# A fused convolution and gated MLP: the first block's chain laid anew over the engines, the first weight pieces used for both token halves, loads queued by need, the convolution's output copied from PSUM by ScalarE

## The chip, the cores and the metric

One core of one Trainium2 chip. The metric is the device time of one execution in microseconds (us); lower is better. In the profile PE is TensorE (PEld its weight loads), DVE is VectorE, ACT is ScalarE, POOL is GpSimd, SP is SyncE, which issues nearly all DMAs. A name such as L712 is a line of the kernel.

## The reference

All tensors are bf16, S = 2048 tokens, D = 576, F = 4608.

```python
mod = (silu(c) @ w_mod)                      # six rows of 576: sa, ca, ga, sb, cb, gb
h = layernorm(x) * (1 + ca) + sa             # x is A_q
k_shift = 4-tap causal shift of A_k, taps shift_k
kv = k_shift * A_v
y = causal convolution over all 2048 tokens of kv with ssm_k, per channel (by FFT), + kv * ssm_D
x = x + ga * (h * y)
h = layernorm(x) * (1 + cb) + sb
x = x + gb * ((silu(h @ w1) * (h @ w3)) @ w2)
```

## The kernel before

**Blocks and row blocks.** Tokens go in 8 blocks of 256. The convolution is done per block in a small transform domain: `k_rows` (transpose of the filter's block, L311) and `w_spectrum` give the filter's spectrum W, `v_block` makes V of two neighbouring W, `kv_rows` makes the shifted product kv, `x_spectrum` its spectrum X, `x_sums` one more component, and `pair(X, V, s)` multiplies a block's X with a V and adds the product to block s's accumulator z. A block s needs the pairs of all earlier X, so X and V are kept in DRAM (`Xd`, `Vd`) and read back with `get`. `real_parts` and `inverse` bring z back to tokens (into PSUM), `gate_rows` and `gate` make the modulated layer norm `hg`, `residual` adds `hg * y` to x; then come the second layer norm (`ln_stats`, `normed_act`), `turn` (ten PE transposes) and `turned` (five ACT instructions into `h2T`, the transposed input of the MLP). `outcome` is the sequence from `real_parts` to `turned`.

**The MLP** takes row blocks of 512 tokens (two blocks). `hidden(r, fc, t0, t1, rate)` loads one of nine pieces of w1 and w3 (512 columns of each, `wst`, two buffers, four DMAs) and does four f of 128 columns: 16 matmuls with 128 rows and four with 64, then Silu (L726) and a copy (L728) on ACT and a product on DVE (L729). `down` multiplies by w2 (four buffers, 18 DMAs) into two PSUM tiles and adds to x. There are four PSUM tiles in all (`ps`), shared by everything.

**Order of the work.** `first_block` brings block 0 to `h2T` alone; the order of its DVE, ACT and PE instructions is the program's (`in_order`). In it stand the modulation rows too (`mod_piece` 2, 1, 0, 5 and `mod_columns`). Then `hidden` runs for six pieces on block 0's 256 tokens (`N1 = 24` f) while block 1's convolution (`conv_second`) is interleaved; then row block 0 runs pieces 6 to 8 on 512 tokens and pieces 0 to 5 once more, with weights loaded again, on tokens 256 to 512; then `down`. The convolution of blocks 2r+2 and 2r+3 (`conv`) is interleaved with row block r. The interleaving is by a budget: each step of the convolution yields a cost, `advance` adds a share of time after every f or group of down matmuls (`rate`, from `CONV_US`), and steps are issued while the budget is positive. A negative cost is room that `mix` fills with other steps. Beyond that a scheduler orders instructions when it compiles; it may move an instruction ahead of earlier ones on its engine where its inputs allow.

**Loads.** All large loads are issued by SP. In block 0: k, filter, v, x, then w_mod in two halves (`load_mod`), the next block's filter, k and v, spill of V, x of block 1, weight pieces 0 and 1, spill of X, x of blocks 2 and 3, four pieces of w2. POOL issues c, D and two small pieces of k.

Of the kernel before, what the change touches and what calls it, by code (L numbers as in the profile page):

```python
# [29 lines left out]
CONV_US = (86.5, 93.5, 109.5)  # L30
N1 = 24
# [9 lines left out]
class _Kernel:  # L41
    def __init__(self, ctx, tc, q, k, v, shift_k, ssm_k, ssm_D, w1, w3, w2, c, w_mod, out):
# [21 lines left out]
        self.n_w13 = 0  # L64
# [5 lines left out]
    def setup(self):  # L70
# [51 lines left out]
    def load_mod(self, m):  # L122

        nc = self.nc
        cols = slice(m * D, (m + 3) * D)
        dst = _ap(self.h3, m * D, [[6 * D, 4], [1, 3 * D]])
        nc.sync.dma_start(dst, self.w_mod[0:512, cols].rearrange("(a p) d -> p a d", p=P))
        nc.sync.dma_start(self.wm[0:64, 4 * 6 * D + m * D:4 * 6 * D + (m + 3) * D],
                          self.w_mod[512:D, cols])

    def angles(self, which):

        nc = self.nc
        ang = self.acc.tile([P, 2, 2, 2, P], I32, name="ang", tag=f"z{which}")
        for x in range(2):
            for cs in range(2):
                nc.vector.tensor_scalar(ang[:, x, cs], self.arow_i[:],
                                        self.acol[:, 2 * which + x:2 * which + x + 1],
                                        512.0 * (1 - cs), op0=ALU.mult, op1=ALU.add)
        nc.vector.tensor_single_scalar(ang[:], ang[:], 2047, op=ALU.bitwise_and)  # L140
        self.ang = self.ang if hasattr(self, "ang") else {}
        self.ang[which] = ang

# [41 lines left out]
    def mod_piece(self, m):  # L185
        nc = self.nc
        w5 = self.wm[:, 0:5 * 6 * D].rearrange("p (a d) -> p a d", a=5)
        ps = self.ps()
        for h, ct in [(h, ct) for h in range(2) for ct in range(4)] + [(0, 4), (1, 4)]:
            n = P if ct < 4 else 64  # L190
            nc.tensor.matmul(ps[:, h, 0:H], self.crep[0:n, ct, :],  # L191
                             w5[0:n, ct, m * D + h * H:m * D + (h + 1) * H],
# [34 lines left out]
    def load_kv(self, s, between=None):  # L227
        nc = self.nc
        kh = self.ld.tile([P, 5, D], BF16, name="kh", tag="kh")
        if s == 0:  # L230
# [3 lines left out]
            nc.gpsimd.dma_start(kh[1:2, 1:5, :], bass.AP(tensor=self.k.tensor, offset=self.k.offset,  # L234
                                                       ap=[[2 * D, 1], [D, 4], [1, D]]))
            nc.gpsimd.dma_start(kh[0:1, 3:5, :], bass.AP(tensor=self.k.tensor, offset=self.k.offset,
# [615 lines left out]
```

## Time and profile before

| | us |
|---|---|
| runs (3) | 579.86, 579.95, 580.1; median 579.95 |
| profiled execution | 576.23, of which the span is 574.5 |
| PE busy | 527.4 (92% of the span) |
| DVE busy | 322.5 (56%) |
| ACT busy | 299.0 (52%) |
| POOL busy | 47.7 (8%) |
| mean granted TensorE clock | 0.971 |
| DMA | 121.65 MB, 212 GB/s in the mean |

The largest groups of the page (line, engine, operation; busy us, mean ns):

```profile
L712 PE MATMUL ps<-h2T,wst 128*128 128x512 bf16 (+1 forms) x1314 | 268.7, 352 | 8.5 <-DMA wst<-in_B_w_dram 5.5
L753 PE MATMUL ps<-w2t,h 128*128 128x288 bf16 x1152 | 145.6, 288 | 9.2 <-DVE ty L459 3.4
```

A group's row reads: what it writes and reads, shapes, count, then busy time and mean time of one, then the idle time of the engine just before its instructions and what ended most of that. In the rows of waits, `PE ps L712 <- DMA wst` reads: PE stood before line 712 until a DMA into `wst` had landed. PE's matmuls are pipelined and their ends are modelled, so busy PE time is not time at peak rate.

### The profile page before, as it was taken

The page shows a single profiled execution, that of the slowest core. Times are in us where ns is not written, and L with a number is a line of the kernel's source. Part 1 is how long each engine was busy: PE and PEld are TensorE (multiplying, and loading weights), DVE is VectorE, ACT ScalarE, POOL GpSimd, SP SyncE. Part 2 cuts the span into 40 slices and gives each one's busy share as a digit, 9 for nine tenths or more (in the row PEclk, how much of TensorE's full clock was granted, in tenths as well). Part 3 has the DMA queues.
Part 4 walks back from the last instruction along what each step waited for, and adds up shares of the span by engine and source line. Part 5 has one row for each costly group of instructions (what it writes and reads, how often), then busy time and mean ns, then how long its engine had stood idle before and what let it go on. Part 6 is the DMA issues. An engine that isn't in the chain of part 4 may idle for free.

```text
span 574.5 us, 9033 instructions
## 1 busy us (share of the span) xinstructions
PE 527.4 (92%) x3465; PEld 306.3 (53%) x3496; DVE 322.5 (56%) x496; ACT 299.0 (52%) x627; POOL 47.7 (8%) x107
## 2 busy tenths in 40 slices
PE   5779889999998989999898989999899999999996
PEld 2457554466776634434476744333367843334775
DVE  9569936598676238795496137999453032222011
ACT  5757588655724276557723277455663245555100
POOL 3120010000313010001201010000131000000000
PEclk9959989999998999999999999999989999999999
DMA  9996787597896667976978559745245554452353
GB/s 272 364 280 242 233 244 233 182 342 249 309 337 217 184 211 233 317 260 180 330 247 257 145 175 378 250 149 161 91 121 140 145 165 131 127 154 83 85 153 93
DMA packets 104984, 121.65 MB, mean 212 GB/s; under 512 B 5359, under 2 KB 95215, under 8 KB 104942
## 3 DMA queue, kind: packets, MB, share of 16 engines
q1 hardware_dynamic: 104812, 121.07, 66.4%
q8 instruction: 27, 0.44, 0.3%
q14 instruction: 15, 0.12, 0.1%
q0 software_dynamic: 128, 0.01, 0.0%
q10 hardware_dynamic: 2, 0.00, 0.0%
HBM read 107.20 MB, written 13.86 MB: 211 GB/s over the span
## 4 chain that ended last, share of the span: by engine, by line
PE 56%; DVE 18%; DMA 11%; ACT 9%; issue 3%; POOL 3%; SPq 0%; DVEq 0%; ACTq 0%
PE ps L712 25%; PE ps L753 21%; DMA wst<-in_B_w_dram 6%; PE ps L720 4%; DVE z L365 4%; DVE p L363 4%; PE ps L271 3%; ACT junk L377 3%; DVE h L729 2%; ACT sg L726 1%; ACT u L728 1%; DMA V<-Vd 1%; DMA x<-in_A_q_dram 1%; DMA out_dram<-x 1%; PE ps L191 1%
## 5 line engine op out<-in xcount | busy, mean ns | idle before, releaser
L712 PE MATMUL ps<-h2T,wst 128*128 128x512 bf16 (+1 forms) x1314 | 268.7, 352 | 8.5 <-DMA wst<-in_B_w_dram 5.5
L712 PEld LDWEIGHTS <-wst 128*128 128x128 bf16 x1344 | 126.1, 99 | 135.9 <-issue 26.6
L726 ACT ACTIVATE sg<-ps 128x512 bf16<-128x512 f32 (+1 forms) x168 | 90.2, 537 | 138.9 <-PE ps L720 70.8
L753 PE MATMUL ps<-w2t,h 128*128 128x288 bf16 x1152 | 145.6, 288 | 9.2 <-DVE ty L459 3.4
L729 DVE TENSOR_TENSOR h<-sg,u 128x512 bf16<-128x512 bf16 (+1 forms) x168 | 63.7, 382 | 131.8 <-ACT u L728 131.7
L753 PEld LDWEIGHTS <-h 128*128 128x128 bf16 x1152 | 113.0, 98 | 39.5 <-issue 7.3
L728 ACT CAST u<-ps 128x512 bf16<-128x512 f32 (+1 forms) x168 | 87.7, 522 | 0.0
L377 ACT ACTIVATE junk<-x 128x576 bf16<-128x576 bf16 x60 | 41.4, 690 | 45.0 <-DVE x L461 39.1
L363 DVE TENSOR_TENSOR p<-X,V 128x3456 bf16<-128x3456 bf16 x28 | 54.6, 1950 | 2.6 <-DMA V<-Vd 2.5
L761 DVE TENSOR_TENSOR og<-ps,gbrow 128x288 bf16<-128x288 f32 x32 | 13.1, 449 | 74.5 <-PE ps L753 74.5
L365 DVE TENSOR_TENSOR z<-z,p 128x3456 bf16<-128x3456 bf16 x28 | 54.6, 1949 | 0.0
L720 PE MATMUL ps<-h2T,wst 64*128 64x512 bf16 (+1 forms) x336 | 47.3, 352 | 0.2 <-DVE ty L459 0.2
L271 PE MATMUL ps<-kT,Fk 128*128 128x288 bf16 x128 | 20.0, 304 | 7.9 <-ACT u L728 3.9
L720 PEld LDWEIGHTS <-wst 64*128 64x128 bf16 x336 | 10.0, 94 | 31.7 <-issue 31.1
L493 ACT ACTIVATE h2T<-ps,sbcol,cbcol 128x256 bf16<-128x256 bf16 (+1 forms) x43 | 20.0, 552 | 10.6 <-PE ps L478 9.8
L391 POOL TENSOR_SCALAR l2m<-l2s 128x2 f32<-128x2 f32 x7 | 2.1, 295 | 266.8 <-ACT junk L377 266.8
L271 PE MATMUL ps<-kv,Fb 128*128 128x288 bf16 x128 | 19.8, 300 | 4.6 <-ACT u L728 3.8
L473 ACT ACTIVATE h2row<-x,l2n,l2r 128x576 bf16<-128x576 bf16 (+1 forms) x28 | 16.8, 652 | 11.9 <-POOL l2n L396 11.9
L421 ACT ACTIVATE hg<-x,l1n,l1r 128x576 bf16<-128x576 bf16 x16 | 13.3, 867 | 16.8 <-POOL l1n L396 16.8
L271 PEld LDWEIGHTS <-Fk 128*128 128x128 bf16 x128 | 12.8, 104 | 16.0 <-issue 11.5
L450 PE MATMUL ps<-z,Fb 128*128 128x288 bf16 x128 | 18.2, 295 | 3.0 <-DVE z L440 2.9
L274 ACT CAST W<-ps 128x576 bf16<-128x576 f32 x32 | 19.2, 666 | 2.5 <-PE ps L271 2.5
(94 smaller groups left out, 327.6 us busy)
## 6 DMA issues: line engine op xcount, KB each, us to landing
wst<-in_B_w_dram SPq DMA_DIRECT2D x84, 512.0 KB, 5.0
w2t<-in_B_w_dram SPq DMA_DIRECT2D x72, 288.0 KB, 3.3
X<-Xd SPq DMA_DIRECT2D x12, 864.0 KB, 6.7
V<-Vd SPq DMA_DIRECT2D x10, 864.0 KB, 6.1
Vd<-V SPq DMA_DIRECT2D x7, 864.0 KB, 4.5
wst<-in_B_w_dram SPq DMA_DIRECT2D x84, 64.0 KB, 3.0
Xd<-X SPq DMA_DIRECT2D x6, 864.0 KB, 5.2
kh<-in_A_k_dram SPq DMA_DIRECT2D x7, 720.0 KB, 6.1
```

Of the source, the lines that this page charges most:

```text
L271: nc.tensor.matmul(ps[:, h, 0:H], basis[:, cc, cs, e, :], rhs[:, cc, h * H:(h + 1) * H], start=(cc == 0), stop=(cc == 1))
L274: nc.scalar.copy(dst(e, cs).rearrange("p (h d) -> p h d", h=2), ps[:, :, 0:H])
L363: nc.vector.tensor_mul(p[:], X[:], V[:])
L365: nc.vector.tensor_add(z[:], z[:], p[:])
L377: self.nc.scalar.activation(junk[:], src[:, i, :], func, accum_out=out[:, i:i + 1])
L493: nc.scalar.activation(dst, src, ACT.Identity, bias=self.sbcol[:, ct:ct + 1], scale=self.cbcol[:, ct:ct + 1])
L712: nc.tensor.matmul(gus[fi][:, i, 0:n], w[:, 5 * i + ct, fi * P:(fi + 1) * P], hT[:, ct, t0:t1], start=(first and ct == 0), stop=(not first ...
L720: nc.tensor.matmul(gus[fi][:, i, 0:n], w[rows, 4, fi * P:(fi + 1) * P], hT[rows, 4, t0:t1], start=first, stop=not first)
L726: nc.scalar.activation(sg[:, 0:n], gus[fi][:, 0, 0:n], ACT.Silu)
L728: nc.scalar.copy(u[:, 0:n], gus[fi][:, 1, 0:n])
L729: nc.vector.tensor_mul(self.h3[:, f, t0:t1], sg[:, 0:n], u[:, 0:n])
L753: nc.tensor.matmul(accs[t // 2][:, t % 2, 0:H], self.h3[:, f0 + f, t * P:(t + 1) * P], w[:, f, :], start=(f0 + f == 0), stop=(f0 + f == NF ...
```

## The change

It touches the first block, the stage after it, the order of the loads, and the layer-norm and output steps of every later block.

- **Block 0.** The second set of angles is made by POOL, ahead of the identity. The layer-norm sums of its first 128 tokens come earlier on ACT, those of the other 128 from DVE (`quick_stats`). X's sum, the product with V and the real parts are done in two halves on DVE, ahead of `arow` and `brow`. Six warm-up matmuls are dropped, four added. `k_rows(1)` and half of `w_spectrum(1)` move into block 0's last part; `mod_piece(5)` moves out into block 1's convolution, with a load of its own (`load_gb`). The two halves of `h2T` get PSUM tiles of their own.
- **Weights.** `N1 = 28`: seven pieces run on tokens 0 to 256. Pieces 0 and 1 are loaded right after V of block 0; pieces 5 and 6 are then used at once for tokens 256 to 512 (`kept`), pieces 7 and 8 run on 512 tokens, pieces 0 to 4 are loaded again.
- **Loads.** c and the small pieces of k are issued by SP and ACT. The spills of X and V of blocks 0 and 1 move behind pieces 7 and 8. SP's order up to the end of the first stage is the program's.
- **Every block.** ACT copies the inverse out of PSUM into `y`; DVE's two residual steps work on SBUF, 256 tokens at a time. `behind(nc.scalar)` puts the layer-norm sums, gate rows and normed rows behind the ACT instruction traced just before them. `gate_stats` is split off `gate_rows` and stands earlier.

```diff
-CONV_US = (86.5, 93.5, 109.5)
-N1 = 24
+CONV_US = (84.6, 91.6, 107.6)
+RATE1 = 1.31
+N1 = 28
...
         nc.vector.memset(self.one[:], 1.0)
+        self.ang = {}
+        self.angles(nc.gpsimd, 0)
+        make_identity(nc, self.ident[:])
         nc.gpsimd.memset(self.knat[64:P, 4, :], 0.0)
-        make_identity(nc, self.ident[:])
+        nc.gpsimd.memset(self.h2T[0][:, 0, :], 0.0)
...
-        self.load_kv(0, between=lambda: self.load_k(0))
-        nc.gpsimd.dma_start(self.crow[:], self.c)
+        def between():
+            self.load_k(0)
+            nc.sync.dma_start(self.crow[:], self.c)
+            self.load_x(0)
+        self.load_kv(0, between)
         nc.gpsimd.dma_start(self.drow[:], self.ssm_D.rearrange("(o d) -> o d", o=1))
-        self.load_x(0)
-        self.load_mod(0)
-        self.load_mod(3)
-        nc.gpsimd.memset(self.h2T[0][:, 0, :], 0.0)
+        self.load_mod(0, 3)
+        self.load_mod(3, 2)
...
+    def load_gb(self):
+        self.wgb = self.ld.tile([P, 5, D], BF16, name="kh", tag="kh")
...
+    def behind(self, engine):
+        last = [i for i in self.nc.cur_bb.bb.instructions if i.engine == engine.engine][-1]
+        return self.tc.issue_after(last)
...
+    def residual_row(self, s, cc, ps):            # block 0: as before, from PSUM
...
+    def residual(self, s, y):
+        nc.vector.tensor_mul(hg[:], hg[:], y[:])
+        nc.vector.tensor_add(x1[:], x1[:], hg[:])
...
     def first_block(self):
-        self.angles(1)
-        self.angles(0)
+        self.angles(nc.vector, 1)
+        self.whole_turns(1)
+        self.whole_turns(0)
         self.shift_taps()
         self.waves(1)
+        self.waves(0)
         self.warm(4)
         self.run_all(self.k_rows(0))
-        self.waves(0)
+        self.load_k(1)
+        self.warm(4)
...
         self.cond_silu()
+        self.cond()
+        self.ln_sums(x1, 0, sums[0], sums[1], 0)
+        scales = [self.ln_scales(*sums, "l1")]
         self.run_all(self.w_spectrum(0))
-        self.cond()
         self.run_all(rows)
-        self.ln_sums(self.xo[0], 0, *st)
+        mean, rstd = self.quick_stats(x1[:, 1, :], "l1")
...
         self.run_all(self.x_spectrum(0))
         self.run_all(self.v_block(0))
+        self.load_w13(0)
+        self.load_kv(1)
         self.load_x(1)
-        self.mod_piece(2)
-        self.ln_sums(self.xo[0], 1, *st)
-        for m in (1, 0):
+        self.load_w13(1)
+        for o in (0, 3):
+            nc.vector.tensor_add(X[:, o, :], X[:, o + 1, :], X[:, o + 2, :])
+            nc.vector.tensor_mul(z[:, o:o + 3, :], X[:, o:o + 3, :], V[:, o:o + 3, :])
+            nc.vector.tensor_add(z[:, o + 1, :], z[:, o, :], z[:, o + 1, :])
+            nc.vector.tensor_sub(z[:, o, :], z[:, o, :], z[:, o + 2, :])
+        for m in (2, 1, 0):
             self.mod_piece(m)
-        self.gate_rows(0, self.ln_scales(*st, "l1"))
-        self.run_all(self.x_sums(0))
-        self.run_all(self.pair(self.X[0], self.V[0], 0))
-        self.real_parts(0)
-        self.warm(6)
+        for cc in range(2):
+            nc.scalar.activation(hg[:, cc, :], x1[:, cc, :], ACT.Identity, bias=b[:, 0:1], scale=r[:, 0:1])
+        ps = [self.inverse(0, cc) for cc in range(2)]
         self.run_all(self.gate(0))
-        ps = [self.inverse(0, cc) for cc in range(2)]
         self.mod_columns()
+        self.run_all(self.k_rows(1))
+        W1 = self.w_spectrum(1)
         pt = self.ps((P, 2, 1024), BF16)
-        self.residual(0, 0, ps[0])
+        self.residual_row(0, 0, ps[0])
...
-        self.turn(pt, 0)
+        self.turn_split(pt, 0)
+        for _ in range(2):
+            next(W1)
         st.append(self.quick_stats(x1[:, 1, :], "l2"))
-        self.turned(0, pt, 0, 1)
+        self.turned_split(pt, 0, False)
         self.normed(0, 1, *st[1])
-        self.turn(pt, 1)
-        self.turned(0, pt, 1, 1, True)
-        self.mod_piece(5)
+        pt = self.ps((P, 2, 1024), BF16)
+        self.turn_split(pt, 1)
+        self.turned_split(pt, 1, True)
...
     def outcome(self, s, fill=()):
             self.real_parts(s)
             yield 1.5
             yield -3.5
-            ps = [self.inverse(s, cc) for cc in range(2)]
+            y = self.lnp.tile([P, 2, D], BF16, name="y", tag="y")
+            for cc in range(2):
+                nc.scalar.copy(y[:, cc, :].rearrange("p (h d) -> p h d", h=2), self.inverse(s, cc)[:, :, 0:H])
             yield -3.5
-            for cc in range(2):
-                self.residual(s, cc, ps[cc])
-                yield 1.2
-            r, b = self.ln_stats(self.xo[s], "l2")
+            self.residual(s, y)
+            yield 1.5
+            with self.behind(self.nc.scalar):
+                r, b = self.ln_stats(self.xo[s], "l2")
             yield -4.0
-            self.normed_act(s, r, b)
+            with self.behind(self.nc.scalar):
+                self.normed_act(s, r, b)
...
     def conv_second(self):
-        self.gate_rows(1)
-        yield from self.k_rows(1)
-        yield from self.kv_rows(1)
-        yield from self.w_spectrum(1)
-        yield from self.x_spectrum(1)
-        yield from self.gate(1)
+        self.gate_stats(1)
+        yield from self.W1
+        yield from self.kv_rows(1)
+        self.load_gb()
         yield from self.v_block(1)
+        self.gate_rows(1)
+        yield from self.x_spectrum(1)
+        self.mod_piece(5)
...
+        yield from self.gate(1)
         yield from self.outcome(1)
...
     def run(self):
             for fc in range(n1):
-                self.hidden(0, fc, 0, 256, 39.0 / (N1 * 1.03 * 0.8))
+                self.hidden(0, fc, 0, 256, RATE1)
             self.end()
+        sync = self.nc.sync.engine
+        last = self.in_order(0, [sync])[sync]
+        with self.tc.issue_after(last):
+            self.row_blocks(n1)
...
+    def row_blocks(self, n1):
             if r == 0:
-                for fc in range(n1):
+                self.load_kv(2)
+                self.load_k(2)
+                for fc in (n1 - 2, n1 - 1):
+                    self.hidden(0, fc, 256, 512, rate, self.kept[fc])
+                for fc in range(n1, NF // FC):
+                    self.hidden(0, fc, 0, RB, rate)
+                    self.keep_x(fc % 2)
+                    self.keep_v(fc % 2)
+                for fc in range(n1 - 2):
                     self.hidden(0, fc, 256, 512, rate)
```

More of the change, by code (lines that the diff above doesn't have):

```diff
@@ L348, in v_block @@
         self.V[s] = V
[L349 to L350 removed]
+        if 1 < s < NBLK - 1:
+            self.keep_v(s)
         yield 0.75
@@ L479, in turn, with turn_split, turned_split, turned @@
                                      self.h2row[:, cc, ct * P:(ct + 1) * P], self.ident[:])
-    def turned(self, s, pt, c0, n, split=False):
+    def turn_split(self, pt, cc):
+        for ct in range(5):
+            self.nc.tensor.transpose(pt[:, ct // 3, ct % 3 * P:(ct % 3 + 1) * P],
+                                     self.h2row[:, cc, ct * P:(ct + 1) * P], self.ident[:])
+    def turned_split(self, pt, cc, both):
+        hT = self.h2T[0]
+        for ct in range(5):
+            dst, src = hT[:, ct, cc * P:(cc + 1) * P], pt[:, ct // 3, ct % 3 * P:(ct % 3 + 1) * P]
+            if both and ct > 2:
+                self.nc.vector.tensor_scalar(dst, src, self.cbcol[:, ct:ct + 1], self.sbcol[:, ct:ct + 1],
+                                             op0=ALU.mult, op1=ALU.add)
+            else:
+                self.nc.scalar.activation(dst, src, ACT.Identity, bias=self.sbcol[:, ct:ct + 1],
+                                          scale=self.cbcol[:, ct:ct + 1])
+    def turned(self, s, pt, c0, n):
         nc = self.nc
```

132 lines of the change are left out of this document (79 added, 53 removed).

## The prediction

> **What bounds the kernel now.** I read the busy table by stages first: block 0 alone (to 42.2 us), the first halves of six weight pieces (to 84.2), the rest of row block 0's hidden layer (to 152), its down projection (to 195), then row blocks 1 and 2. Columns: stretch, length, busy us (instructions) of PE, PE's weight loads, DVE, ACT and POOL, granted clock, DMA share, GB/s.
>
> ```profile
> 0.00:42.20 42.20, 28.31 (x187) 17.32 (x188) 29.30 (x56) 24.88 (x48) 9.83 (x29) 0.81 0.98 312
> 42.20:84.20 42.00, 37.58 (x313) 26.04 (x314) 32.06 (x57) 29.04 (x78) 3.08 (x6) 0.95 0.73 235
> 84.20:152.00 67.80, 63.92 (x462) 37.74 (x463) 45.82 (x73) 46.23 (x109) 3.46 (x12) 1.00 0.79 260
> 152.00:195.00 43.00, 39.57 (x319) 30.79 (x318) 28.12 (x35) 15.34 (x35) 10.37 (x12) 0.96 0.81 255
> 195.00:327.00 132.00, 122.89 (x773) 67.88 (x780) 83.44 (x113) 71.93 (x144) 9.83 (x24) 1.00 0.74 244
> 327.00:461.00 134.00, 126.60 (x783) 69.87 (x790) 82.27 (x111) 72.89 (x144) 11.09 (x24) 0.97 0.58 178
> ```
>
> After block 0 TensorE is busy 89 to 95% of every stage, so time can come from two places: block 0, where PE idles 13.9 of 42.2 us and the clock is 0.81, and the waits that PE still has. Those are in the waits of PE over the whole span (total, times, longest):
>
> ```profile
> PE ps L271 <- ACT u L728: 7.7, 5, 2.6
> PE ps L712 <- DMA wst<-in_B_w_dram: 5.5, 8, 1.3
> PE ps L753 <- DVE ty L459: 3.4, 2, 2.6
> ...
> PE ps L753 <- ACT u L728: 2.5, 1, 2.5
> ...
> PE ps L712 <- ACT u L728: 1.0, 1, 1.0
> ```
>
> All but the weight wait are waits for one of the four PSUM tiles: 7.7 + 3.4 + 2.5 + 1.0 = 14.6 us, all after 152 us. The waits of ACT say why its evacuations come late; it executes in order, and layer-norm work stood ahead of them, waiting:
>
> ```profile
> ACT junk L377 <- DVE x L461: 39.1, 8, 13.4
> ...
> ACT hg L421 <- POOL l1n L396: 16.8, 6, 4.7
> ```
>
> **Part 1, block 0.** The chain of waits there (start, length), and DVE's wait in it:
>
> ```profile
> 23.81 0.76 DVE brow L205
> 25.27 1.97 DVE z L358
> 27.26 0.77 DVE z L440
> 28.05 0.76 DVE z L441
> 28.81 0.68 DVE hg L432
> 29.51 0.77 DVE hg L434
> 30.38 0.77 DVE ty L459
> ...
> 37.27 1.75 ACT h2T L493 x5
> 39.07 0.69 PE ps L478 x5
> 39.76 2.51 PE ps L191 x10
> 42.27 1.41 PE ps L712 x8
> ```
> ```profile
> DVE arow L203 <- PE ps L191: 4.3, 1, 4.3
> ```
> ```profile
> 18.75 2.24 ACT L274 CAST X<-ps 128x576 bf16<-128x576 f32 x4
> ```
>
> Now DVE idles 4.3 us for the modulation products while X is ready at 18.75 + 2.24 = 21.0, and only afterwards forms the spectral product. After the change the product stands ahead of `arow` and `brow`, in two halves. Two of the four LN sums leave ACT for DVE and the others come before W's copies; I put the last X copy at 19 to 21. One half costs a sum of half L440's size (0.4), half of L358 (1.0) and two steps of half L440's size (0.8): 2.2. The other half lies beside the X copies, so z is final at 21.2 to 23.2 instead of 28.81. `arow`, `brow` and the two gate steps (4 x 0.76 = 3.0) follow on DVE; the inverse transform runs on PE beside them. The first residual starts at 24.4 to 26.4 instead of 30.38: 4 to 6 us earlier. I take 4.5.
>
> From residual to first hidden matmul it is now 42.2 - 30.4 = 11.8 us. Out go `mod_piece(5)` (2.51) and part of the second turn's wait for ACT (a PSUM tile of its own). In come, on the same in-order engines, block 1's ten transposes, ACT's kT copy and two groups of W(1) with their copies (0.56 each, the X copies' 2.24 / 4; kT is of two such): about 3 on PE at the cold clock, partly in its gaps, and 2.2 on ACT, ahead of ACT's five L493. Net -0.5, between +2 and -3. Dropping six warm-up matmuls and adding four earlier can leave the inverse at half clock as it is today; nothing gained or lost. ACT issues the two small `kh` loads before its first work: nothing. POOL's angles: below.
>
> Sum of part 1: **-5.0** (-1.5 to -7.5); first hidden matmul near 37.
>
> **Part 2, from there to 152.** One unblocked f takes, by the spacing of the Silu rows, 1.09 us for 256 tokens and 2.04 for 512:
>
> ```profile
> 117.78 0.38 ACT L726 ACTIVATE sg<-ps 128x256 bf16<-128x256 f32 x1 [0.34 <-PE ps L712]
> ...
> 118.87 0.38 ACT L726 ACTIVATE sg<-ps 128x256 bf16<-128x256 f32 x1 [0.45 <-PE ps L720]
> ```
> ```profile
> 248.20 0.60 ACT L726 ACTIVATE sg<-ps 128x512 bf16<-128x512 f32 x1 [0.98 <-PE ps L720]
> ...
> 250.24 0.60 ACT L726 ACTIVATE sg<-ps 128x512 bf16<-128x512 f32 x1 [0.97 <-PE ps L712]
> ```
>
> Four more f are split, 4 x (2.18 - 2.04) = +0.5. The ten matmuls of L191 above took 2.51 at half clock, so one takes 0.125 warm, and ten transposes 0.7 (L478: five in 0.69 cold). The convolution's PE work in stage 1 thus loses the transposes and half of W(1), -0.7 - 8 x 0.125, and gains `mod_piece(5)`, 10 x 0.125: -0.5.
>
> Stage 1 idles 42.0 - 37.58 = 4.4 now, and its clock of 0.95 costs some 2.1 more: 6.5, on weights, on LN waits and on cold stretches. What it will lose: SP's queue is now in program order, so piece 2 of w1/w3 (1.18 MB) stands behind the 0.66 MB for `gb`, which waits for `kv_rows(1)` on DVE; at block 0's 312 GB/s both take 6 us against the 5 that PE spends on a piece with its share of convolution: 1, and 0.5 for their issue. Each us that `kv_rows(1)` is late is one more. The step costs sum to 37.65 while 28 advances of 1.343 give 37.6, so the last step (turn and five L493) falls behind the last f, and the second halves that follow need it: five L493 took 1.75 for one half, so about 2.4 for two, 2.5. A cold start: 0.8. In all 4.8 instead of 6.5: -1.7.
>
> Pieces 5 and 6 serve both halves without a reload, so one piece less is read; in exchange four spills (0.88 MB each) come into the third stage. That moved 67.8 us x 260 GB/s = 17.6 MB; +3.5 - 1.2 makes 295 GB/s, under the 312 that block 0 moved. So the spills stay covered, narrowly; without that cover they cost 2.3 MB / 0.3 = 8 us. The weight wait of 5.5 neither grows nor shrinks in my sum.
>
> Sum of part 2: +0.5 - 0.5 - 1.7 = **-1.7** (+2 to -5).
>
> **Part 3, the PSUM waits after 152.** In `outcome` ACT copies the inverse to SBUF (4 x 0.56 more a row block) and DVE works there afterwards, so PSUM no longer waits for DVE's L459 behind 1.95 us products: of 3.4 I take 2.5. LN sums, gate rows and normed rows are bound behind the ACT instruction issued last, so they no longer stand ahead of Silu with a wait of their own. For the other 11.2 I take half, 5.5, since ACT's order is still strict and gains the copies. **-8.0** (-2 to -13). The two planner rates only follow these step costs.
>
> **Sum:** -5.0 - 1.7 - 8.0 = -14.7. The profiled execution took 576.23 (span 574.5 and 1.7 around it): 561.5. The median of the runs lies 3.7 above it: 579.95 - 14.7 = **565.2**. All bounds together give 554.5 to 578.5.
>
> **The rivals.** *POOL is late.* Block 0's second set of angles moves to POOL, ahead of the identity that the transposes need. The rows that bear on it:
>
> ```profile
> 23.43 0.20 POOL L394 TENSOR_TENSOR l1v<-l1v,l1r 128x2 f32<-128x2 f32 x1
> ```
> ```profile
> 281.13 1.95 DVE L363 TENSOR_TENSOR p<-X,V 128x3456 bf16<-128x3456 bf16 x1
> 281.35 1.79 POOL L394 TENSOR_TENSOR l1v<-l1v,l1r 128x2 f32<-128x2 f32 x1
> ```
>
> The same 2-element POOL instruction takes 0.20 alone and 1.79 beside a DVE product, until that ends. If the four angle instructions are held so by DVE's own four, and are slow themselves, the angles end about 2 us later than DVE could use them, and DVE, which masks them before the tap work, idles for that: part 1 shrinks to -3, the time is 567.2. The Trainium skill (SBUF — State Buffer, Who interferes with whom) states it as a lock: VectorE and GpSimd share one port pair, and whoever starts second is blocked for the whole instruction; the trace agrees (1.79 against 0.20).
>
> *Front alone.* The PSUM waits come back elsewhere: PE is fast enough to fill four tiles whenever ACT does any long step. For it: ACT's work grows. Against it: ACT is busy only 54% in the two long stages (71.93 of 132, 72.89 of 134). Gain 5.0 + 1: 574.
>
> *All of it.* The 14.6 nearly vanish and stage 1 flows: -7 - 4 - 14: 555.
>
> *Slower.* The y copy is one more in-order step on ACT that waits for PE's inverse, and that for DVE's z. Today's eight waits of ACT for L461 (39.1, the longest 13.4) show how far such a step can stand still; Silu behind it would stop PE at all seven outcomes. It decides from 14.7 / 7 = 2.1 us each; at 3.5 each the time is 590. Against it: the inverse is issued 3.5 units after `real_parts`, and PE shows no wait for z outside block 0.
>
> **Chances.** Forecast 0.50 (its own range 559 to 571); POOL late 0.15; front alone 0.14; all of it 0.09; slower 0.08; gains and losses cancel to within 0.2% (1.2 us, about what these runs can tell from no change) 0.04. Faster 0.88, same 0.04, slower 0.08. A range of 555 to 575 leaves out about 2 in 10: the slow case, a few of the best, some of the front alone.
>
> **What would show it.** Right: first hidden matmul near 37, z ahead of `arow`, the first halves done near 79 with four more f, no PE wait for a residual, ACT's 39.1 gone. Wrong: PE waits on ACT of over 2 us after an inverse, weight waits over 8 in total, a DMA share near 1 in the third stage, or a hidden start after 40.

## The result, and the profile after

The changed kernel takes 565.01 us (median of 562.72 to 566.88), the kernel before in the same comparison 579.9 (579.44 to 580.1): ratio 0.9742, 95% interval 0.9706 to 0.9779. Its profiled execution took 565.24, the span is 563.5. In later comparisons the kernel before had medians of 577.09 to 580.06, so kernels of different comparisons are set against each other by their ratios. The stages below are those of one execution each.

The lines of the changed kernel: residual L497/L498 (L492 in block 0), y copy L675, LN sums L398, normed rows L510, turn L515, `turned` L543 (L532 in block 0), gate and up matmuls L796 and L804, Silu L810, u L812, down L837, weight loads L769/L770.

The busy table by stages of before, cut where the first hidden matmul and the first down matmul of each row block start (columns as in the prediction). Shown are the hidden layer and the down projection of row block 0, and those of row blocks 1 and 2:

```profile
42.21:150.49 108.28, 100.38 (x766) 63.00 (x770) 76.48 (x127) 73.75 (x182) 6.53 (x18) 0.98 0.76 248
150.49:194.84 44.35, 40.52 (x327) 31.46 (x325) 29.35 (x37) 16.85 (x38) 10.37 (x12) 0.96 0.81 260
194.84:284.00 89.16, 85.39 (x463) 38.04 (x470) 58.09 (x82) 58.30 (x116) 7.91 (x17) 1.00 0.75 253
284.00:327.45 43.45, 38.12 (x317) 30.29 (x315) 25.97 (x34) 13.63 (x28) 1.92 (x7) 1.00 0.72 225
327.45:422.39 94.94, 87.54 (x454) 38.52 (x461) 70.16 (x88) 59.46 (x116) 5.00 (x13) 0.96 0.58 188
```

The same view of after, with block 0 ahead:

```profile
0.00:34.43 34.43, 25.74 (x194) 16.53 (x195) 27.99 (x56) 19.84 (x36) 10.59 (x27) 0.89 0.88 260
34.43:149.07 114.64, 103.05 (x796) 66.19 (x796) 76.77 (x130) 80.28 (x209) 11.18 (x27) 0.96 0.80 255
149.07:195.46 46.39, 41.49 (x328) 31.95 (x328) 29.00 (x35) 17.36 (x34) 6.82 (x9) 0.96 0.81 261
195.46:282.48 87.02, 85.86 (x473) 38.23 (x471) 58.90 (x82) 61.42 (x122) 5.57 (x18) 1.00 0.78 260
282.48:323.44 40.96, 38.27 (x317) 30.28 (x315) 23.73 (x31) 12.86 (x28) 1.85 (x6) 1.00 0.77 236
323.44:410.68 87.24, 85.07 (x462) 37.67 (x460) 67.26 (x84) 58.02 (x116) 5.45 (x18) 1.00 0.63 205
```

Block 0 ends 7.8 us sooner (34.43 for 42.21). Row block 0's hidden layer is 6.4 longer (114.64 for 108.28) and its down projection 2.0 longer, so that row block 1 starts at 195.46 where it started at 194.84: the whole front is given back. Row block 1 then gains 4.6 and row block 2 7.2; the rest is unchanged. In the span that is 11.0.

The waits of PE of after over the whole span (total, times, longest):

```profile
PE ps L796 <- DMA wst<-in_B_w_dram: 6.9, 6, 2.0
PE ps L515 <- ACT h2row L510: 6.1, 5, 4.0
...
PE ps L837 <- DMA w2t<-in_B_w_dram: 2.8, 3, 1.8
PE ps L796 <- ACT h2T L532: 2.3, 1, 2.3
PE ps L796 <- ACT h2T L543: 1.9, 4, 1.3
PE ps L837 <- ACT u L812: 1.4, 2, 1.2
```

The waits for PSUM tiles (14.6 before) are nearly gone, waits for u of 1.4 (down) and 0.9 (L285, the convolution) are left; in their place stand waits for the normed rows and for h2T, nearly all in row block 0. PE's longest waits there after the first hidden matmul, of after (start, length; in brackets the idle time before and what ended it; the rows between them are left out):

```profile
62.26 0.61 PE L796 MATMUL ps<-h2T,wst 128*128 128x256 bf16 x4 [1.17 <-DMA wst<-in_B_w_dram]
75.11 0.61 PE L796 MATMUL ps<-h2T,wst 128*128 128x256 bf16 x4 [2.01 <-DMA wst<-in_B_w_dram]
80.16 0.56 PE L515 MATMUL ps<-ident,h2row 128*128 128x128 bf16 x5 [0.96 <-ACT h2row L510]
83.11 0.27 PE L796 MATMUL ps<-h2T,wst 128*128 128x256 bf16 x1 [1.30 <-ACT h2T L543]
128.18 0.61 PE L796 MATMUL ps<-h2T,wst 128*128 128x256 bf16 x4 [1.36 <-DMA wst<-in_B_w_dram]
142.55 0.61 PE L796 MATMUL ps<-h2T,wst 128*128 128x256 bf16 x4 [1.36 <-DMA wst<-in_B_w_dram]
182.60 0.56 PE L515 MATMUL ps<-ident,h2row 128*128 128x128 bf16 x5 [3.97 <-ACT h2row L510]
```

Three places: weights in both halves of the hidden layer; the end of stage 1 (the first halves, to 83.1), where block 1's turn comes too late for the second halves; and block 3's turn in the down projection.

### The profile page after: what moved, and what is told of

Same layout as the page of the kernel before. It is cut to its first block, busy times and chain, and to the rows that moved or that the text cites. A ratio compares the mean times of both kernels' runs of the same rounds, so it can differ in the third digit from the quotient of the medians.

```text
span 563.5 us, 9126 instructions
## 1 busy us (share of the span) xinstructions
PE 527.3 (94%) x3534; PEld 308.3 (55%) x3534; DVE 317.9 (56%) x490; ACT 305.2 (54%) x645; POOL 43.4 (8%) x111
## 4 chain that ended last, share of the span: by engine, by line
PE 71%; ACT 11%; DMA 9%; DVE 5%; issue 3%; POOL 2%; SPq 0%; DVEq 0%; ACTq 0%; POOLq 0%
PE ps L796 38%; PE ps L837 19%; PE ps L804 6%; DMA wst<-in_B_w_dram 5%; PE ps L285 4%; DMA w2t<-in_B_w_dram 3%; ACT junk L398 3%; PE ps L482 2%; ACT sg L810 1%; ACT h2row L510 1%; ACT u L812 1%; ACT X L288 1%; PE ps L333 1%; ACT W L288 1%; ACT hg L453 1%
## 5 line engine op out<-in xcount | busy, mean ns | idle before, releaser
L796 PE MATMUL ps<-h2T,wst 128*128 128x512 bf16 (+1 forms) x1376 | 271.9, 347 | 12.3 <-DMA wst<-in_B_w_dram 6.9
L796 PEld LDWEIGHTS <-wst 128*128 128x128 bf16 x1376 | 129.0, 98 | 138.9 <-issue 30.7
L810 ACT ACTIVATE sg<-ps 128x512 bf16<-128x512 f32 (+1 forms) x172 | 91.2, 530 | 142.0 <-PE ps L804 86.2
L837 PE MATMUL ps<-w2t,h 128*128 128x288 bf16 x1152 | 145.8, 288 | 4.3 <-DMA w2t<-in_B_w_dram 2.8
L837 PEld LDWEIGHTS <-h 128*128 128x128 bf16 x1152 | 113.1, 98 | 34.6 <-issue 5.4
L812 ACT CAST u<-ps 128x512 bf16<-128x512 f32 (+1 forms) x172 | 88.5, 515 | 1.2 <-DVE h L813 1.1
L804 PE MATMUL ps<-h2T,wst 64*128 64x512 bf16 (+1 forms) x344 | 47.4, 349 | 0.0
L398 ACT ACTIVATE junk<-x 128x576 bf16<-128x576 bf16 x58 | 39.9, 689 | 10.7 <-DVE x L498 10.2
L804 PEld LDWEIGHTS <-wst 64*128 64x128 bf16 x344 | 10.1, 94 | 31.5 <-issue 30.4
L675 ACT CAST y<-ps 128x576 bf16<-128x576 f32 x14 | 8.9, 643 | 29.8 <-PE ps L482 29.7
L413 POOL TENSOR_SCALAR l1m<-l1s 128x2 f32<-128x2 f32 x7 | 3.0, 428 | 247.7 <-ACT junk L398 247.7
L510 ACT ACTIVATE h2row<-x,l2n,l2r 128x576 bf16<-128x576 bf16 (+1 forms) x28 | 16.1, 657 | 10.0 <-POOL l2n L418 10.0
L285 PE MATMUL ps<-kv,Fb 128*128 128x288 bf16 x128 | 18.8, 285 | 2.4 <-ACT X L288 1.1
L543 ACT ACTIVATE h2T<-ps,sbcol,cbcol 128x256 bf16<-128x256 bf16 x35 | 16.8, 584 | 7.8 <-PE ps L515 7.8
L285 PE MATMUL ps<-kT,Fk 128*128 128x288 bf16 x128 | 20.0, 306 | 0.5 <-DVE kT L589 0.5
L288 ACT CAST X<-ps 128x576 bf16<-128x576 f32 x32 | 19.0, 671 | 2.3 <-PE ps L285 2.3
L305 DVE TENSOR_TENSOR kv<-kv,kvt 128x1152 bf16<-128x1152 bf16 x24 | 18.1, 754 | 0.3
```

The costliest lines, as they stand in the source:

```text
L285: nc.tensor.matmul(ps[:, h, 0:H], basis[:, cc, cs, e, :], rhs[:, cc, h * H:(h + 1) * H], start=(cc == 0), stop=(cc == 1))
L288: nc.scalar.copy(dst(e, cs).rearrange("p (h d) -> p h d", h=2), ps[:, :, 0:H])
L398: self.nc.scalar.activation(junk[:], src[:, i, :], func, accum_out=out[:, col:col + 1])
L510: self.nc.scalar.activation(row[:, cc, at:at + hi - lo], x1[:, cc, lo:hi], ACT.Identity, bias=b[:, cc:cc + 1], scale=r[:, cc:cc + 1])
L796: nc.tensor.matmul(gus[fi][:, i, 0:n], w[:, 5 * i + ct, fi * P:(fi + 1) * P], hT[:, ct, t0:t1], start=(first and ct == 0), stop=(not first ...
L804: nc.tensor.matmul(gus[fi][:, i, 0:n], w[rows, 4, fi * P:(fi + 1) * P], hT[rows, 4, t0:t1], start=first, stop=not first)
```

## The experiments

Theory 1 was that the front's gain is all lost inside row block 0 and the gain at the end comes from the later blocks' edits alone; theory 2 that both parts reach the end. The stages of all kernels, in us (profiled execution), and the ratio to before:

| kernel | block 0 | hidden 0 | down 0 | row block 1 | row block 2 | rest | ratio (95%) |
|---|---|---|---|---|---|---|---|
| before | 42.2 | 108.3 | 44.3 | 132.6 | 133.3 | 113.7 | 1 |
| after | 34.4 | 114.6 | 46.4 | 128.0 | 126.1 | 113.9 | 0.9742 (0.9706–0.9779) |
| late_only | 42.8 | 111.9 | 43.3 | 127.9 | 126.1 | 113.7 | 0.9828 (0.9779–0.9876) |
| front_only | 39.1 | 110.9 | 39.4 | 134.0 | 135.3 | 113.9 | 0.9909 (0.9878–0.994) |
| no_y | 34.9 | 111.3 | 47.3 | 125.2 | 126.0 | 113.9 | 0.9725 (0.9679–0.9771) |
| no_behind | 39.2 | 109.9 | 49.8 | 127.5 | 130.0 | 113.9 | 0.9848 (0.9789–0.9907) |
| rate1 | 34.9 | 107.4 | 44.5 | 126.8 | 126.1 | 114.0 | 0.9631 (0.959–0.9672) |
| conv0 | 34.8 | 117.9 | 40.2 | 126.3 | 126.1 | 113.9 | 0.9734 (0.9691–0.9777) |
| warm2 | 34.8 | 115.5 | 46.7 | 125.8 | 126.1 | 114.0 | 0.9788 (0.9746–0.983) |
| spill0 | 34.5 | 117.4 | 46.9 | 129.6 | 126.1 | 113.9 | 0.9845 (0.9787–0.9902) |
| nw3 | 35.1 | 106.3 | 62.0 | 136.6 | 131.0 | 121.1 | 1.0207 (1.017–1.0245) |
| best1 | 34.7 | 109.0 | 42.1 | 128.8 | 126.1 | 113.9 | 0.9581 (0.9544–0.9619) |
| best2 | 35.0 | 110.5 | 39.2 | 126.2 | 126.0 | 114.0 | 0.9536 (0.9497–0.9576) |
| rate18 | 35.2 | 109.8 | 46.6 | 125.9 | 126.1 | 114.0 | 0.9665 (0.9634–0.9696) |

**late_only: the later blocks' edits on the kernel before.**

```diff
-CONV_US = (86.5, 93.5, 109.5)
+CONV_US = (84.6, 91.6, 107.6)
...
-            ps = [self.inverse(s, cc) for cc in range(2)]
...
+            for cc in range(2):
...
+                nc.scalar.copy(y[:, cc, :]..., self.inverse(s, cc)[:, :, 0:H])
...
+            with self.behind(self.nc.scalar):
+                r, b = self.ln_stats(self.xo[s], "l2")
...
```

> The kernel before with only the edits of the later blocks: ScalarE copies both inverse results out of PSUM (y), the layer-norm and its normed rows are put behind the engine's last instruction, the gate's statistics are split from its rows, and the three convolution paces are those of the change. The loads, block 0's order over the engines and the six split pieces (24 f) stay as before. Theory 1 (the front's 7.8 us are all given back inside row block 0; the gain at the end comes from the later edits): within 3 us of the changed kernel, 562 to 568 us. Theory 2 (the front's gain reaches the end and the later edits add a part): 570 to 573 us, between the two kernels. In the trace, by both: the 39.1 us that ACT waited for the row sum at the residual are gone, and PE's waits for a PSUM tile behind u after row block 0 fall from 7.7 + 2.5 + 1.0 to under 3; by theory 1 the starts of row blocks 2 and 3 lie within 3 us of the changed kernel's 323.4 and 449.5.

Measured: 567.59 us, before 577.96 in the same comparison; 1.7% faster, some 10 us. The time alone lies at the edge of theory 1, but before was 2 us lower here too: 0.9828 of 579.9 is 569.9, at the edge of theory 2. In the trace ACT waits 11.0 for the row sum at the residual, not 39.1, and PE's waits behind u after row block 0 are 0.9 + 0.2, as both theories had it; the starts of row blocks 2 and 3 (325.9 and 452.0) lie 2.5 behind those of after, which is within theory 1's bound. Row blocks 1 and 2 gain 4.7 and 7.2, as in after. But row block 1 starts at 198.0, 3.2 later than in before: the later edits cost time in row block 0 by themselves, where PE waits 6.8 for weights in the hidden layer (4.4 in before) and 2.5 for the normed rows (1.6).

**front_only: the front alone.**

```diff
-CONV_US = (84.6, 91.6, 107.6)
+CONV_US = (86.5, 93.5, 109.5)
...
-        return self.tc.issue_after(last)
+        return contextlib.nullcontext()
...
-            self.residual(s, y)
-            yield 1.5
+                self.residual_row(s, cc, ps[cc])
+                yield 1.2
...
+        self.gate_rows(s0)
         yield from self.kv_rows(s0)
         yield from self.v_block(s1)
-        self.gate_rows(s0)
...
```

> The changed kernel with only its front: block 0's order, the loads in program order and 28 split f stay; the later blocks' convolution results are read out of PSUM by VectorE again, nothing is put behind an engine's last instruction, the gate's statistics and rows are formed together at their old places, and the three paces are those of before. Theory 1: the first hidden matmul stays near 34.4, but row block 1 starts near 195 as in both kernels, and the time is 575 to 580 us. Theory 2: 570 to 573 us, with row block 1 starting before 192.

Measured: 572.99, before 577.96; 0.9% faster, some 5 us (574.6 of 579.9, between the two ranges). Row block 1 starts at 189.3, 5.5 sooner than in before. The two parts' gains (0.91% and 1.72%) add up to 2.63%, after's is 2.58%. So theory 1 falls: the front alone is faster, by an interval clear of 1. It is not the earlier start that arrives, though. When the hidden layer ends only 0.5 of it is left (149.94 for 150.49); the other 5.0 come in the down projection (39.4 for 44.3), where PE waits for no residual (3.4 in before) and the clock is 1.00 for 0.96. Row blocks 1 and 2 then give 1.4 and 2.0 back, with 14.5 us of waits behind u from 150 us on (11.2 in before). Of the 6.1 us between the starts of row block 1 in front_only and in after, 3.2 are what the later edits cost by themselves; the rest arises only where both are together, and its cause is open. The first hidden matmul stands at 39.1, not at 34.4: 4.7 of the earlier start were due to `behind`, as no_behind shows.

**no_y: blocks 1 to 7 multiplied out of PSUM by VectorE again, two residual steps.** (The expectation names blocks 1 to 3; the edit stands in `outcome`, which all later blocks run.)

```diff
-            y = self.lnp.tile([P, 2, D], BF16, name="y", tag="y")
+            ps = [self.inverse(s, cc) for cc in range(2)]
+            yield -3.5
             for cc in range(2):
...
-                nc.scalar.copy(y[:, cc, :]..., self.inverse(s, cc)[:, :, 0:H])
-            yield -3.5
-            self.residual(s, y)
-            yield 1.5
+                self.residual_row(s, cc, ps[cc])
+                yield 1.2
...
```

> The changed kernel, but the two inverse results of blocks 1 to 3 are again multiplied out of PSUM by VectorE, half by half, with two residual steps in place of ScalarE's copies y and one residual. Theory 'the order counts' (what held PE was ACT waiting at the layer-norm's row sum, and putting that work behind ACT's queue removes it): +1 to +3 us on the changed kernel, PE waiting 1 to 3 us more for a PSUM tile that a residual holds. Rival 'the copy counts' (the PSUM tiles held until VectorE came): +6 us or more, with PE's waits for the residual back at 3.4 or above.

Measured: 562.36, ratio 0.9725, the same as after within the intervals, where both theories had it slower. The copy by ScalarE is worth nothing here. Two waits of no_y, of ACT and of PE:

```profile
ACT junk L398 <- DVE x L492: 33.4, 5, 12.0
PE ps L835 <- DVE hg L490: 1.0, 2, 0.7
```

ACT waits for the residual 33.4 us again (39.1 before, 10.2 in after), and PE loses 1.0 to a residual. The total of ACT's wait was no measure of what it costs PE. That it counts what is queued behind the waiting instruction is the reading that no_behind supports.

**no_behind: y kept, no step bound behind an engine's last instruction.**

```diff
-        return self.tc.issue_after(last)
+        return contextlib.nullcontext()
```

> The changed kernel, but no step is put behind an engine's last instruction: gate statistics, gate rows, layer-norm and normed rows stand where the program order puts them; y stays. Theory 'the order counts': +6 to +9 us on the changed kernel, ACT again waiting 20 us or more at the junk row sum for the residual x, and PE's waits behind u near 8. Rival 'the copy counts': within 2 us of the changed kernel.

Measured: 570.54, ratio 0.9848: 1.06% over after, some 6 us, as the order theory has it. Its number for ACT was a miss: ACT waits 12.4 at that row sum, not 20 or more. But PE's waits behind u are back, near the 8 expected: 6.1 before L285 and 1.0 before L796 from 150 us on (11.2 in before, 1.1 in after). PE's two largest waits of no_behind there:

```profile
PE ps L515 <- ACT h2row L510: 7.5, 2, 7.1
PE ps L285 <- ACT u L812: 6.1, 5, 1.9
```

So ACT waits little here and PE much, and in no_y the other way round: the order on ACT is what counts. In block 0 the trace shows what `behind` did there; ACT and PE of no_behind (rows between them left out):

```profile
31.96 0.68 ACT L398 ACTIVATE junk<-x 128x576 bf16<-128x576 bf16 x1
34.40 1.62 ACT L453 ACTIVATE hg<-x,l1n,l1r 128x576 bf16<-128x576 bf16 x2 [1.66 <-POOL l1n L418]
35.93 1.15 ACT L288 CAST W<-ps 128x576 bf16<-128x576 f32 x2
...
35.38 0.71 PE L521 MATMUL ps<-ident,h2row 128*128 128x128 bf16 x5 [3.66 <-DVE h2row L435]
39.23 2.30 PE L796 MATMUL ps<-h2T,wst 128*128 128x256 bf16 x8 [3.15 <-ACT h2T L532]
```

Without it block 1's layer-norm sums and gate rows are scheduled ahead of W's copies and block 0's own h2T. The hidden layer still ends at 149.2, as in after (149.1) and front_only (149.9): of an earlier start of 4.8 nothing is left there. The 6.9 by which the span is longer than after's lie in the down projection of row block 0 (3.4) and in row block 2 (3.9).

**warm2: ten idle matmuls ahead of the first hidden one.**

```diff
+        wps = self.ps()
+        for _ in range(10):
+            self.nc.tensor.matmul(wps[:, 0, 0:256], self.ident[:], self.Fb[:, 0, 0]..., start=True, stop=True)
         self.turned_split(pt, 1, True)
```

> The changed kernel with ten more matmuls of 256 columns, whose result nothing reads, between the second turn of block 0 and the first hidden matmul, where TensorE waited 2.3 us for h2T at a granted clock of 0.50. Theory (the 5.6 us after the start ran at half clock because TensorE had idled just before, so 2.8 us are lost to the clock): the clock between 34.4 and 40 us rises from 0.50 to 0.75 or more, the row block's hidden layer becomes 1.5 to 2.8 us shorter, and as much reaches the end. Rival (the weights' two buffers set the pace of stage 1): the clock rises, the weight waits before 80 us grow by as much from 3.2, and the time stays within 0.8 us.

The same stretch in after and in warm2, and PE's rows of warm2 with a weight wait before 80 us (the rows between them left out):

```profile
34.40:40.00 5.60, 5.56 (x25) 2.83 (x25) 4.12 (x8) 3.57 (x10) 0.00 (x0) 0.50 0.02 4
```
```profile
34.40:40.00 5.60, 5.16 (x43) 3.18 (x41) 4.39 (x9) 4.21 (x12) 0.00 (x0) 0.98 0.02 4
```
```profile
48.58 0.61 PE L799 MATMUL ps<-h2T,wst 128*128 128x256 bf16 x4 [1.11 <-DMA wst<-in_B_w_dram]
50.56 0.61 PE L799 MATMUL ps<-h2T,wst 128*128 128x256 bf16 x4 [0.56 <-DMA wst<-in_B_w_dram]
62.06 0.61 PE L799 MATMUL ps<-h2T,wst 128*128 128x256 bf16 x4 [1.20 <-DMA wst<-in_B_w_dram]
73.21 0.61 PE L799 MATMUL ps<-h2T,wst 128*128 128x256 bf16 x4 [0.74 <-DMA wst<-in_B_w_dram]
74.95 0.61 PE L799 MATMUL ps<-h2T,wst 128*128 128x256 bf16 x4 [1.14 <-DMA wst<-in_B_w_dram]
```

The clock rises to 0.98, PE does 43 matmuls there instead of 25 (the last of the fillers among them), and weight waits before 80 us rise from 3.2 to 4.75; the hidden layer is 115.5 for 114.6. One can follow the gain: block 1's transform of kv (L285) starts at 45.44 for 47.20, 1.8 sooner, and behind the first two of these waits PE is 0.2 ahead (52.86 for 53.07, the same matmuls). The ratio is 0.9788, no faster than after's 0.9742, with overlapping intervals. The rival holds: what PE gains at the start of stage 1 it gives to the weights.

**spill0: block 0's spectra spilled right behind block 0.**

```diff
         self.W1 = W1
+        self.keep_x(0)
+        self.keep_v(0)
...
-                    self.keep_x(fc % 2)
-                    self.keep_v(fc % 2)
+                    if fc % 2:
+                        self.keep_x(1)
+                        self.keep_v(1)
```

> The changed kernel, but block 0's two spectra (0.88 MB each) are spilled right behind block 0, where the DMA engines were busy 0.02 to 0.30 of the time from 30 to 42 us, and only block 1's in the third stage. Theory (the weight waits at 128 and 130 us, 2.0 together, are the late spills on a full DMA, whose share was 1.01 to 1.05 from 115 to 130): those waits go and the time falls by 1.5 to 2.5 us; nothing is added before 60. Rival (they come from the two weight buffers and not from the amount of data): the waits stay between 1.5 and 2.5 and the time within 0.8 us.

Measured: 568.18, ratio 0.9845, against 0.9742 of after: slower by 1%, which neither theory had. PE's weight waits of the third stage stay, 3.3 in all, as in after (1.36 + 0.59 + 1.36):

```profile
123.57 0.61 PE L798 MATMUL ps<-h2T,wst 128*128 128x256 bf16 x4 [0.59 <-DMA wst<-in_B_w_dram]
125.58 0.61 PE L798 MATMUL ps<-h2T,wst 128*128 128x256 bf16 x4 [1.39 <-DMA wst<-in_B_w_dram]
138.13 0.61 PE L798 MATMUL ps<-h2T,wst 128*128 128x256 bf16 x4 [1.31 <-DMA wst<-in_B_w_dram]
```

So 1.77 MB less in that stage bought nothing: these waits do not come from the amount of data. Why it is slower stays open; its clock in the hidden layer was 0.93 for 0.96.

**nw3: a third buffer for the pieces of w1/w3**, on no_y, the room taken from w2's buffers.

```diff
-NW13 = 2
+NW13 = 3
...
-NW2 = 4
+NW2 = 2
```

> The kernel no_y with a third buffer for the weight pieces of w1/w3; the room for it comes from the buffers of w2, two instead of four. Theory (stage 1 and the second halves are held by the two weight buffers: a piece's load can start only when the piece two before it is used up): PE's waits for w1/w3 before 150 us fall from 5.9 to under 2, the hidden layer of row block 0 from 111.3 to 107 to 109; the down projections may each lose a few us to w2, which would hide that at the end, so the stage is what is read. Rival (the DMA engines or the queue's order are the limit, not the buffers): the waits stay above 4.

PE's waits of nw3, the first in the hidden layer of row block 0, the second from 203 us on:

```profile
PE ps L794 <- DMA wst<-in_B_w_dram: 1.2, 2, 0.7
...
PE ps L835 <- DMA w2t<-in_B_w_dram: 18.4, 22, 4.1
```

The weight waits fall from 5.9 to 1.2 (before 83 us from 2.6 to 1.2, behind it from 3.3 to none) and the hidden layer from 111.3 to 106.3, below the theory's number: the two buffers hold that stage. In the second halves the buffers are not the only difference, since two pieces of w2 instead of four are loaded from 108 us on. The price at w2 was far over "a few us" (down projections 62.0, 54.1, 46.6 and 49.7 us), so 591.16 in all says nothing about the third buffer.

**rate1: block 1's steps spread over fewer of the 28 split f.**

```diff
-RATE1 = 1.31
+RATE1 = 1.55
```

> The changed kernel with RATE1 1.55 instead of 1.31: the convolution steps of block 1, its turn among them, are spread over fewer of the 28 split f, so that the turn no longer falls behind the last of them. Theory (stage 1's tail, PE waiting for h2row and h2T between 79 and 86 us, is a matter of pace): PE waits for h2T and h2row before 90 us fall from 5.7 to under 2.5, the hidden layer of row block 0 takes 111 to 113 us instead of 114.6, and the time falls by 2 to 3.4 us. Rival (block 1's chain over VectorE is the limit there, not its pace): the same waits, the same time within 1 us.

Measured: 555.19, ratio 0.9631, 1.1% under after, twice to three times what was expected. PE's waits in the hidden layer of row block 0 of rate1:

```profile
PE ps L796 <- DMA wst<-in_B_w_dram: 2.6, 5, 1.3
PE ps L796 <- ACT h2T L532: 2.4, 1, 2.4
PE ps L515 <- ACT h2row L510: 1.4, 1, 1.4
```

The turn comes at 71.6 instead of 80.2 and the wait for h2T L543 is gone. What is left before 90 us, 2.4 + 1.4, is over the 2.5 expected, but 2.4 of it is the first hidden matmul's wait, which the pace does not touch. The weight waits fell too, from 6.5 to 2.6, which I had not expected. The likely reason, which the rows fit and no run isolates: with more convolution beside each of the first pieces, PE stays on a piece as long as the next one's load takes. Some 1.1 us of this execution are not the edit's: its clock from 34.4 to 40 us was 0.70 for 0.50 (an estimate, 5.6 x 0.2), in work that the edit leaves as it was. best1, with the same pace and a clock of 0.50 there, has no weight wait at all up to 95 us. PE also does not cool down at the end of stage 1; the clock from 85 to 90 us is 1.00 in rate1 and 0.67 in after.

**rate18: fewer still.**

```diff
-RATE1 = 1.31
+RATE1 = 1.8
```

> The changed kernel with RATE1 1.8: block 1's steps over some 21 of the 28 split f. If the pace of 1.55 has removed the tail and stretched each piece over its load already: within 1.5 us of that kernel's 0.963 of before, or up to 2 us slower, since the last two pieces then run without convolution beside them and wait for weights again. If the steps' lateness is still the limit: another 2 us or more faster.

Measured: ratio 0.9665, 0.3% over rate1 with overlapping intervals. Stage 1's weight waits are back (1.36 at 58.0, 1.08 at 72.0), so the faster pace brings nothing more; whether it costs something, these runs do not tell.

**conv0: blocks 2 and 3 sooner.**

```diff
-CONV_US = (84.6, 91.6, 107.6)
+CONV_US = (96.0, 91.6, 107.6)
```

> The changed kernel with CONV_US[0] 96 instead of 84.6: the convolution steps of blocks 2 and 3 come about an eighth sooner under row block 0's second part. Theory (the 4.5 us that PE waited at 182.6 for block 3's normed rows is a matter of order: the steps come too late for ACT and POOL to be done): the wait falls below 1, the down projection of row block 0 takes 41 to 43 us instead of 46.4, the time falls by 3 to 5 us. Rival (block 3's chain is bound by VectorE, whose products were running back to back before it): the wait stays over 3 us and the time within 1.5 us.

The chain of block 3's turn in after, then in conv0 (its rows alone):

```profile
175.62 1.96 DVE L377 TENSOR_TENSOR p<-X,V 128x3456 bf16<-128x3456 bf16 x1 [0.40 <-DMA X<-Xd]
175.69 1.96 POOL L413 TENSOR_SCALAR l2m<-l2s 128x2 f32<-128x2 f32 x1 [25.22 <-ACT junk L398]
177.61 1.96 DVE L379 TENSOR_TENSOR z<-z,p 128x3456 bf16<-128x3456 bf16 x1
177.74 1.88 POOL L415 TENSOR_TENSOR l2r<-l2m 128x2 f32<-128x2 f32 x1
181.67 2.29 ACT L510 ACTIVATE h2row<-x,l2n,l2r 128x576 bf16<-128x576 bf16 x4 [5.26 <-POOL l2n L418]
```
```profile
170.31 0.22 POOL L413 TENSOR_SCALAR l2m<-l2s 128x2 f32<-128x2 f32 x1 [23.76 <-ACT junk L398]
170.62 0.20 POOL L415 TENSOR_TENSOR l2r<-l2m 128x2 f32<-128x2 f32 x1
173.71 0.56 PE L515 MATMUL ps<-ident,h2row 128*128 128x128 bf16 x5 [1.32 <-ACT h2row L510]
```

In after POOL's two small steps start beside a long DVE step each and take 1.96 and 1.88 instead of 0.22 and 0.20; the six steps together take 6.0 instead of 2.4. ACT stands 5.26 for them and PE 3.97. In conv0 they meet none, PE waits 1.9 in all for h2row, and the down projection takes 40.2 instead of 46.4. The Trainium skill (SBUF — State Buffer, Who interferes with whom) calls that an exclusive lock of the port pair that VectorE and GpSimd share; the trace agrees. My number for the wait (below 1) was a miss. The order theory holds for the stall; but the hidden layer is 3.2 longer (117.9), the profiled execution 4.4 shorter, and the ratio, 0.9734, is that of after within the intervals. The time, expected 3 to 5 lower, was a miss too: how much of the 6.2 reaches the end stays open.

**best1 and best2: both paces together, with y and without it.** best2 has no_y's edit besides.

```diff
-CONV_US = (84.6, 91.6, 107.6)
-RATE1 = 1.31
+CONV_US = (90.0, 91.6, 107.6)
+RATE1 = 1.55
```

> The changed kernel with RATE1 1.55 and CONV_US[0] 90.0: both paces of row block 0 together. If the two are separate stalls: 2 to 4 us under the kernel with RATE1 1.55 alone, 551 to 553.5 us, with the down projection of row block 0 at 41 to 43 us instead of 44.5. If the sooner steps only move the stall into the hidden layer: within 1.5 us of it.

> best1 without ScalarE's copies y (VectorE multiplies blocks 1 to 3 out of PSUM). If y is worth nothing, as it was with the changed kernel's paces: within 1.5 us of best1; if the sooner steps make VectorE's chain the limit, y pays now: 2 us or more slower than best1.

Measured on one chip: 556.05 and 552.45 (before 580.06). best1's down projection is 42.1, as expected; its ratio lies 0.5% under rate1's, or 2.9 us as expected, but the intervals overlap. best2 is the fastest version run: ratio 0.9536, interval 0.9497 to 0.9576, below the whole intervals of after and of rate1. Leaving y out costs nothing here either. It was 3.6 faster than best1, which neither case of the expectation had, and best1's interval (0.9544 to 0.9619) overlaps; its down projection is 39.2 for 42.1, its hidden layer 110.5 for 109.0.

## Why the prediction was right, and where it was not

The time came out as forecast (565.0 for 565.2), and that was luck: the terms did not. Between the profiled executions, on whose rows the terms were worked out, the change is 11.0 (574.5 to 563.5) and not 14.7: part 2 was 8.1 too good, parts 1 and 3 were 2.8 and 1.6 too cautious, 3.7 in all. Between the medians the change is 14.9 because the profiled execution of before lay 3.7 under its median, that of after at its median. That these two differences are alike is chance. The part that was right in kind is that both block 0 and the waits for PSUM give time.

- **Part 1, block 0: -5.0 forecast, -7.8 measured**, just past its bound of -7.5. z came ahead of `arow`, and the first residual started at 24.87 for 30.38 (`24.87 0.76 DVE L490 TENSOR_TENSOR hg<-ps,hg`). The rest is the way from the residual to the first hidden matmul, where I had -0.5 and the trace has -2.3 (9.56 for 11.8). The undersized piece is `behind`, which I had costed only after 152: without it the start is at 39.2, so that the rest of the front gives 3.0 there.
- **Part 2: the step that failed.** Forecast -1.7 (+2 to -5), measured +6.4 to 149.07; the first halves were done at 83.1, not near 79. By the recipe of the prediction stage 1 loses 48.67 - 42.18 = 6.5 idle and 0.06 x 42.18 = 2.5 by the clock: 9.0, where I had 4.8. The place was wrong for `gb` (no weight wait before 62 us, though SP stood 13.7 for its tile) and the size for the rest: 3.2 for weights by the two buffers, 1.5 and 1.3 for the turn and h2T, 2.5 instead of 0.8 for the cold start. The stage after it lost some 3.5 more: it should have been 66.3 - 4 x (2.04 - 1.09) = 62.5 with four f fewer, and took 65.97, with 3.3 of weight waits for 2.3 and a clock of 0.97 for 1.00 (0.03 x 60.87 = 1.8) after the tail. I had let the weight wait stand at 5.5; it is 6.9. What I missed is the time of a load. I had set bytes over 312 GB/s, 6 us for piece 2 with `gb`, against 5 of work on a piece, and had priced no other piece; those 5 are in no row (42.0 / 6 is 7.0 in the mean). In after the fifth and the seventh piece took 6.3 and 7.2 us from their first DMA's issue (55.88 and 67.90) to the landing that PE waited for (62.2 and 75.1). With two buffers such a load starts only when the piece two before is used up, and the piece between, with no convolution beside it, lasts PE 4 x 1.09 = 4.4: hence the waits of 1.17 and 2.01. A split f gives PE only half as long per piece, and so a sooner or faster PE waits for weights, as warm2 and nw3 show.
- **The spills** were rightly put as covered: spill0 left the waits as they were. The DMA share near 1 that I had named as a sign against me was there (0.99 and 1.03 from 95 to 130 us) and was not the cause of these waits.
- **Part 3: -8.0 forecast, -9.6 measured** from 149.07 on (+2.0 in down 0, -4.6, -7.2, +0.2). The waits for PSUM fell further than forecast, from 14.6 to 2.3 where 6.6 were to stay, and the reason given was half wrong: I put 2.5 on y, which is worth nothing beside `behind` (no_y). In down 0 a wait of 3.97 + 0.53 came for the normed rows, the one over 2 us after an inverse that I had named as a sign of error. It is not the binding that brings it: without it, in no_behind, PE waits 7.5 there.
- **POOL is late** (0.15): the four angles took 2.01 beside DVE's 1.82, and DVE masked them at 3.86 without waiting, so not in block 0. The same lock did strike at block 3's turn, for which I had no term; in before too, two of the six steps there took 2.31 and 1.94.
- **Front alone** (574) is excluded by late_only: the later edits keep 1.7%. **All of it** came true in the waits for PSUM, but stage 1 did not flow. **Slower**: of the seven outcomes only block 3's held PE for over 2 us in one wait.

## What to carry to other kernels

An earlier start is worth only what the next limit lets through: before counting it, read from the trace how long a weight piece's load takes from issue to landing, work out from the buffers how long each piece must then be worked on, and give the interleaved work a pace that fills that time. A long wait of an engine that works in order costs only what is queued behind it, so bind late work behind what others need rather than trying to shorten the wait. When several stages change, judge each from its own rows: a right total can be two wrong terms.

## What the hardware showed that was not expected

- PE worked 5.6 us without a gap at a granted clock of 0.50 (34.40 to 40.00); from 40 to 42 it was 0.87, then 1.00. Ten filler matmuls in the 2.3 us gap before it brought 0.98. The Trainium skill (TensorE: Matmul & The Clock Gate, Part 1: The HAM clock gate) speaks of some 3.4 us of sustained work until the full clock, counted in windows that run on by themselves; here it took some 6 us.
- It was not that gap which had lowered the clock. In after it was 1.00 until 26 us, 0.72 from 26 to 28 and 0.50 from 28 on, while PE is shown at work without a gap from 21.5 to 28.2, most of it (23.25 to 26.97) on the 60 one-column matmuls of `mod_columns`. Whether such matmuls count as too little work for the clock, no run here tests.
- The kernel before had medians from 577.09 to 580.06 in four comparisons, with single times from 573.56 to 581.73: a single profiled execution is no base for terms of 2 or 3 us.
